# Where the edge columns of a transform are loaded and multiplied, in a kernel that overlaps an FFT mixer with an MLP

## The chip, the cores and the metric

The kernel runs on one core of one Trainium2 chip. The metric is the time of one execution in device microseconds (us). A core has five engines that run their own instruction streams: TensorE (PE) multiplies matrices, with its weight loads (PEld) beside it; VectorE (DVE), ScalarE (ACT) and GpSimd (POOL) do elementwise work and copies; SyncE (SP) issues transfers. ScalarE and GpSimd issue transfers too, and each issue takes its place in that engine's stream. Transfers between memory and the on-chip buffers are done by 16 DMA engines. Matmul results land in PSUM and are copied from there by ScalarE or VectorE.

## The reference

What is computed is a gated mix of two branches and the gradients of all its inputs but one. Cut to what matters:

```python
def _A_ref(x, w_r, w_i):                      # spectral branch
    X = rfft2(x.astype(float32)) * (w_r + 1j * w_i)
    return irfft2(X, s=(S, D)).astype(bfloat16)

def _B_ref(x, w1, b1, w2, b2):                # MLP branch
    h = relu(x @ w1 + b1)
    return (h * h) @ w2 + b2

g = sigmoid((x * gate_w).sum(-1, keepdims=True))
out = g * _A_ref(x, w_r, w_i) + (1 - g) * _B_ref(B_x, w1, b1, w2, b2)
# outputs: out, and the vjp with grad_out for A_x, A_w_r, A_w_i, B_w1, B_b1, B_w2, B_b2, gate_w
```

S = 2048 rows, D = 1024 columns, F = 3584 hidden units, bfloat16. The MLP branch is far the larger part; the spectral branch, forward and backward, is done in three stages of matmuls against constant matrices, and these are put in among the MLP's matmuls.

## The kernel before

Python generators write the program. `mlp_grads` writes the weight gradients: 7 groups of 512 hidden units for one weight, 7 for the other, each group 8 products of 16 matmuls (`pw`), one `yield` after each product. `fft_mid` (second stage of the transform: along the rows, the product with the spectral weights, and back) and `fft_out` (third stage) yield after each of their pieces, and `spread` puts these pieces between the products:

```python
def spread(main, side, per_main, start=0.0):
    due, done = start, 0
    for _ in main:
        due += per_main
        while done < due:
            next(side, None)
            done += 1
        yield

def spectra():
    yield from fft_mid()
    yield from fft_out()

spec, grads = spectra(), mlp_grads()
next(grads), next(grads)
todo = 9 + 6 * (R1 // 2) + 2 * NT
for _ in spread(grads, spec, todo / (2.0 * FG * FGC * NH - 2)):
    pass
```

A product of `mlp_grads` (line 816 of the kernel is the `mm`, line 820 the copy):

```python
pw = mps.tile([P, H], FP32, name="pw", tag="pw", bufs=2)
for t in range(NT):
    mm(pw[:], lhsT=cur[:, t, fb_ * P : (fb_ + 1) * P], rhs=dbn[:, t, hf * H : (hf + 1) * H],
       start=(t == 0), stop=(t == NT - 1))
last = nc.scalar.copy(out=wo[:, hf * H : (hf + 1) * H], in_=pw[:])
```

The second stage of the transform begins with the loads of its constants and of the first rows. `ld` issues on SyncE's queue, `st` on GpSimd's:

```python
ld, st = nc.sync.dma_start, nc.gpsimd.dma_start
...
am = fb.tile([P, NM, 2, P], FDT, name="am", tag="am")
ld(out=am[:], in_=cten["am"].ap())            # line 308, 1 MB
bm = fb.tile([P, NM, 2, P], FDT, name="bm", tag="bm")
ld(out=bm[:], in_=cten["bm"].ap())            # line 310, 1 MB

def inputs(m):                                # rows of the pair m, and their spectral weights
    z = fb.tile([P, 2, 2, H], FDT, name="z", tag="z", bufs=2)
    for n, c in enumerate((m, R1 // 2 + m)):
        for x in range(2):
            ld(out=z[lanes[x], n], in_=z_scr[:][c, :, x ^ n if m else x])     # line 316
    wn = ...                                  # four more ld, lines 320
    return z, wn
```

One column in 512 cannot be handled with its row pair and is treated by itself, for all 16 pairs at once: the edge columns. They are loaded element by element (16 pairs x 64 rows, one float16 each, per load), arranged, multiplied in 32 small matmuls with 4 columns, and put into place in `x` of each pair later:

```python
def edges():
    ed = ...; low = ...; mid = ...            # [P, NM, 2, 4], [P, NM, 4], [P, 4]
    col = z_scr[:].rearrange("c r x t l -> r c (x t) l")[:, :, :, 0]
    for e in range(4):
        nc.scalar.dma_start(out=ed[lanes[0], :, 0, e], in_=col[:, 0:NM, e])     # line 341
        nc.scalar.dma_start(out=low[lanes[1], :, e], in_=col[:, NM:, e])        # line 342
    nc.scalar.dma_start(out=mid[lanes[0]], in_=col[:, NM])                      # line 343
    nc.vector.tensor_copy(out=ed[lanes[0], :, 1, :], in_=ed[lanes[0], :, 0, :])
    nc.vector.tensor_copy(out=ed[lanes[0], 0, 1, :], in_=mid[lanes[0]])         # line 345
    ...                                       # four more small copies from low, lines 348, 349
    nc.vector.memset(ed[lanes[1], 0], 0.0)                                      # line 350
    sp = tps.tile([P, NM, 2, 4], FP32, name="sp", tag="tr", bufs=2)
    for m in range(NM):
        for n in range(2):
            mm(sp[:, m, n], lhsT=am[:, m, n, :], rhs=ed[:, m, n, :], ...)       # line 354
    ex = ...                                  # four copies out of sp, line 358
    return ex

def transform(m, n, pm, x):
    px = fps.tile([P, 2, H], FP32, name="px", tag="ps2", bufs=2)
    for T in range(2):
        mm(px[:, T, :], lhsT=am[:, m, n, :], rhs=pm[:, n, T, :], start=True, stop=True)  # line 375
    ...                                       # two copies out of px on ScalarE

nxt = inputs(0)
ex = edges()
pm, w = mirrored(0, nxt[0]), by_groups(nxt[1])
nxt = inputs(1)
held = gs = None
for _ in range(3):
    yield
for m in range(NM + 1):
    if m < NM:
        x = fb.tile([P, 2, 2, LW], FDT, name="x", tag="x", bufs=2)
        for n in range(2):
            transform(m, n, pm, x)
            yield
        nc.vector.tensor_copy(out=x[:, :, :, 0::H], in_=ex[:, m])               # line 473
    ...                                       # products with the weights, back transform (pv), outputs
```

The third stage, `fft_out`, works on tiles of 128 rows: load `r` (ScalarE's queue), `rf` on VectorE, matmuls `pki`, copy `rt`, matmuls `pui`, and elementwise work that ends in `ax_scr`. The `grp` tiles of the weight gradients are loaded with transposing transfers on SyncE's queue.

Of the kernel before, what the change touches and what calls it, by code (L numbers as in the profile page):

```python
# [135 lines left out]
def kernel(  # L136
# [22 lines left out]
    nc = tc.nc  # L159
# [8 lines left out]
    R1, R2 = g.R1, g.R2  # L168
    NT = S // P
# [8 lines left out]
    ld, st = nc.sync.dma_start, nc.gpsimd.dma_start  # L178
# [11 lines left out]
    def pool(name, side="left", space=SBUF, stack=None, bufs=1):  # L190
        stack = ExitStack() if stack is None else stack
        kw = {} if space == DRAM else dict(side=side, reuse_waits="tile")
        return stack.enter_context(tc.tile_pool(name=name, bufs=bufs, space=space, **kw)), stack

    pers, _ = pool("pers", stack=ctx)
    dram, _ = pool("dram", space=DRAM, stack=ctx)
# [105 lines left out]
    def fft_mid():  # L302
        fb, fbs = pool("f2", "right")
        NM, G = R1 // 2, nc.gpsimd
        lanes = [slice(R2 * n, R2 * (n + 1)) for n in range(2)]
# [6 lines left out]
        def inputs(m):  # L312
# [3 lines that stand above are left out]
                    ld(out=z[lanes[x], n], in_=z_scr[:][c, :, x ^ n if m else x])  # L316
            wn = fb.tile([P, 2, LW], BF16, name="wn", tag="wn", bufs=2)
            for c_, src_w in enumerate((A_w_r, A_w_i)):
                for n, k in enumerate(pair_of(m, R1)):
                    ld(out=wn[lanes[n], c_, 0:W1], in_=every(src_w, k))  # L320
            return z, wn

        def by_groups(wn):

            w = fb.tile([P, 3, LW], BF16, name="w", tag="w", bufs=2)
            G.tensor_copy(
                out=w[:, 0:2, 0:H].rearrange("p c (g i) -> p c g i", g=4),
                in_=wn[:, :, 0:H].rearrange("p c (i g) -> p c g i", g=4),
            )
            G.tensor_copy(out=w[:, 0:2, H], in_=wn[:, :, H])  # L330
            G.tensor_scalar(out=w[:, 2, 0:W1], in0=w[:, 1, 0:W1], scalar1=-1.0, scalar2=None, op0=ALU.mult)
            return w

        def edges():

            ed = fb.tile([P, NM, 2, 4], FDT, name="ed", tag="ed")
            low = fb.tile([P, NM, 4], FDT, name="low", tag="low")
            mid = fb.tile([P, 4], FDT, name="mid", tag="mid")
            col = z_scr[:].rearrange("c r x t l -> r c (x t) l")[:, :, :, 0]
            for e in range(4):  # L340
                nc.scalar.dma_start(out=ed[lanes[0], :, 0, e], in_=col[:, 0:NM, e])  # L341
                nc.scalar.dma_start(out=low[lanes[1], :, e], in_=col[:, NM:, e])
            nc.scalar.dma_start(out=mid[lanes[0]], in_=col[:, NM])
            nc.vector.tensor_copy(out=ed[lanes[0], :, 1, :], in_=ed[lanes[0], :, 0, :])
            nc.vector.tensor_copy(out=ed[lanes[0], 0, 1, :], in_=mid[lanes[0]])
            for n in range(2):
                a, b = slice(2 * n, 2 * n + 2), slice(2 - 2 * n, 4 - 2 * n)
                nc.vector.tensor_copy(out=ed[lanes[1], :, n, a], in_=low[lanes[1], :, a])
                nc.vector.tensor_scalar(out=ed[lanes[1], :, n, b], in0=low[lanes[1], :, b], scalar1=-1.0, scalar2=None, op0=ALU.mult)
            nc.vector.memset(ed[lanes[1], 0], 0.0)  # L350
# [3 lines that stand above are left out]
                    mm(sp[:, m, n], lhsT=am[:, m, n, :], rhs=ed[:, m, n, :], start=True, stop=True, skip_group_check=True)  # L354
            ex = fb.tile([P, NM, 2, 2, 2], FDT, name="ex", tag="ex")
            for n in range(2):
                for c in range(2):
                    nc.vector.tensor_copy(
                        out=ex[lanes[n], :, c], in_=sp[lanes[c], :, n, :].rearrange("p m (e t) -> p m t e", e=2)
                    )  # L360
            return ex

        def mirrored(m, z):

            if m == 0:
                return z
            pm = fb.tile([P, 2, 2, H], FDT, name="pm", tag="pm", bufs=2)
            V(out=pm[:, 0], in0=z[:, 0], in1=z[:, 1], op=ALU.add)
            V(out=pm[:, 1], in0=z[:, 0], in1=z[:, 1], op=ALU.subtract)
            return pm  # L370
# [4 lines that stand above are left out]
                mm(px[:, T, :], lhsT=am[:, m, n, :], rhs=pm[:, n, T, :], start=True, stop=True)  # L375
            for c in range(2):
                nc.scalar.copy(out=x[lanes[n], c, :, 0:H], in_=px[lanes[c]])  # L377
# [28 lines left out]
        def back(m, y, ye):  # L406
            pc = fb.tile([P, 2, 2, H], FDT, name="pc", tag="pc", bufs=2)
            for n in (1, 0):
                pv = fps.tile([P, 2, H], FP32, name="pv", tag="ps2", bufs=2)
                for T in range(2):  # L410
                    mm(pv[:, T, :], lhsT=bm[:, m, n, :], rhs=y[:, n, T, 0:H], start=True, stop=True)  # L411
                if m == 0:
                    nc.scalar.copy(out=pc[:, n], in_=pv[:])
                elif n == 1:
                    vc = fb.tile([P, 2, H], FP32, name="vc", tag="vc")
                    nc.scalar.copy(out=vc[:], in_=pv[:])
                else:
                    V(out=pc[:, 0], in0=pv[:], in1=vc[:], op=ALU.add)
                    V(out=pc[:, 1], in0=pv[:], in1=vc[:], op=ALU.subtract)
                yield  # L420

            sp = tps.tile([P, 2, 2], FP32, name="si", tag="tr", bufs=2)
            for n in range(2):
                mm(
                    sp[:].rearrange("p a t -> p (a t)"), lhsT=bm[:, m, n, :], rhs=ye[:, n].rearrange("p a t -> p (a t)"),
                    start=(n == 0), stop=(n == 1), skip_group_check=True,
                )
            nc.vector.tensor_copy(out=pc[lanes[1], 0, :, 0], in_=sp[lanes[0], 0, :])
            if m:
                nc.vector.tensor_copy(out=pc[lanes[0], 1, :, 0], in_=sp[lanes[1], 1, :])  # L430
            else:
                nc.vector.tensor_copy(out=pc[lanes[1], 1, :, 0], in_=sp[lanes[0], 1, :])
            for n, c in enumerate((m, R1 // 2 + m)):
                for h in range(2):
                    st(out=y_scr[:][c, :, h ^ n if m else h], in_=pc[lanes[h], n])
# [22 lines left out]
                    st(out=every(dst_w, k), in_=gw[lanes[n], c_, 0:W1])  # L458

        nxt = inputs(0)  # L460
        ex = edges()
        pm, w = mirrored(0, nxt[0]), by_groups(nxt[1])
        nxt = inputs(1)
        held = gs = None
# [2 lines left out]
        for m in range(NM + 1):  # L467
            if m < NM:
                x = fb.tile([P, 2, 2, LW], FDT, name="x", tag="x", bufs=2)
                for n in range(2):  # L470
                    transform(m, n, pm, x)
                    yield
                nc.vector.tensor_copy(out=x[:, :, :, 0::H], in_=ex[:, m])
            if held:
                backs = back(m - 1, *held)
                next(backs)
                yield
            if m < NM:
                ts = products(x, w)
            if held:  # L480
                next(backs)
                grads_out(m - 1, gs)
                yield
                for _ in backs:
                    pass
            if m < NM:
                held = joined(m, *ts)
                yield
                gs = grads_of_w(x)
                if m + 1 < NM:  # L490
                    pm, w = mirrored(m + 1, nxt[0]), by_groups(nxt[1])
                if m + 2 < NM:
                    nxt = inputs(m + 2)
                for _ in range(1 if m else 3):
                    yield
# [764 lines left out]
# [3 lines that stand above are left out]

    spec, grads = spectra(), mlp_grads()
    next(grads), next(grads)
    todo = 9 + 6 * (R1 // 2) + 2 * NT
    for _ in spread(grads, spec, todo / (2.0 * FG * FGC * NH - 2)):
        pass
    tps_s.close()
# [45 lines left out]
```

## Time and profile before

| | |
|---|---|
| time, median of three executions | 1284.11 us (1283.38 to 1285.54) |
| span of the profiled execution | 1283.1 us |
| ScalarE, busy | 503.4 us (39%) |
| VectorE, busy | 709.3 us (55%) |
| edge loads: number, to landing (`ed`, median) | 9, 3.8 us |
| edge matmuls: number, duration of one (median) | 32, 166 ns |
| first `pw` matmul of the weight gradients | 446.56 us |

The profile page gives each engine's busy time and a strip of 40 slices of the span, with one digit of busy tenths for each slice (9 is 90% or more) and one for the clock that TensorE was granted. The list of waits names, for each instruction that had its engine idle, what ended the idle time. The timeline lists instructions in order of start, neighbours of one kind merged. Matmuls of TensorE overlap, so a single one lasts 379 ns in the trace while the next begins about 216 ns after it.

### The profile page before, as it was taken

How to read it: one execution, taken by the hardware profiler on the slowest of the kernel's cores; microseconds unless marked ns; L12 is line 12 of the kernel's file. 1: busy time of each engine (PE TensorE's matmuls, PEld its weight loads, DVE VectorE, ACT ScalarE, POOL GpSimd, SP SyncE). 2: the span in 40 equal slices, each digit the busy share in tenths (PEclk: the TensorE clock that was granted, in tenths of full speed). 3: DMA queues.
4: the chain of work that ended last, by engine and by line, in shares of the span. 5: the costliest groups of instructions: out<-in, count | busy, mean ns of one | idle time of the engine just before them, and what ended most of it. 6: DMA issues, size and time to landing. Idle time of an engine off the chain costs nothing.

```text
span 1283.1 us, 18411 instructions
## 1 busy us (share of the span) xinstructions
PE 1257.8 (98%) x6884; PEld 610.0 (48%) x6884; DVE 709.3 (55%) x1602; ACT 503.4 (39%) x793; POOL 273.2 (21%) x424
## 2 busy tenths in 40 slices
PE   9999999999999979999999999999999999999997
PEld 5555544555544434444444444455445444444443
DVE  3554433544482206766765762343776776896573
ACT  4756654666633314554555552344111211011100
POOL 0111111111100115545545632122010010000000
PEclk9999999999999989999999999999999999999999
DMA  9566353546454679998778669995899877566540
GB/s 287 202 182 181 132 156 124 178 149 189 104 136 113 154 182 199 222 267 199 186 180 191 134 165 260 256 250 180 223 233 215 211 189 207 155 187 181 162 117 33
DMA packets 326260, 233.27 MB, mean 182 GB/s; under 512 B 195308, under 2 KB 279434, under 8 KB 325914
## 3 DMA queue, kind: packets, MB, share of 16 engines
q1 hardware_dynamic: 282528, 141.17, 47.0%
q0 software_dynamic: 26144, 82.47, 19.3%
q10 hardware_dynamic: 17498, 8.45, 2.7%
q8 instruction: 54, 0.88, 0.3%
q14 instruction: 36, 0.29, 0.1%
HBM read 106.19 MB, written 81.81 MB: 147 GB/s over the span
## 4 chain that ended last, share of the span: by engine, by line
PE 61%; DVE 4%; DMA 2%; issue 1%; ACT 1%; ACTq 1%; SPq 0%; DVEq 0%
PE pw L832 14%; PE acc L906 14%; PE pw L816 12%; PE xX L1015 7%; PE xV L1015 3%; PE pd L685 3%; PE ph L675 3%; PE xZ L1015 2%; DMA grp<-dhT_scr 1%; PE pui L294 1%; PE pki L529 1%; PE px L375 1%; PE pv L411 1%; ACTq L341 1%; ACT x L377 0%
## 5 line engine op out<-in xcount | busy, mean ns | idle before, releaser
L675 PE MATMUL ph<-xT,w1g 128*128 128x512 bf16 x896 | 221.1, 379 | 1.2 <-DMA w1g<-in_B_w_dram 1.2
L685 PE MATMUL pd<-dbT,w2T 128*128 128x512 bf16 x896 | 211.3, 379 | 0.4 <-DVE dhT L689 0.4
L816 PE MATMUL pw<-dbn,grp 128*128 128x512 bf16 x896 | 202.6, 382 | 0.9 <-ACT wo L820 0.4
L832 PE MATMUL pw<-grp,res 128*128 128x512 bf16 x896 | 200.9, 379 | 0.0
L906 PE MATMUL acc<-w,hblk 128*128 128x512 bf16 x896 | 198.7, 379 | 0.0
L689 DVE SCALAR_TENSOR_TENSOR dhT<-pd,rT 128x512 bf16<-128x512 f32 x112 | 77.4, 691 | 202.9 <-PE pd L685 162.9
L816 PEld LDWEIGHTS <-grp 128*128 128x128 bf16 x896 | 87.3, 98 | 108.1 <-issue 6.4
L685 PEld LDWEIGHTS <-w2T 128*128 128x128 bf16 x896 | 87.1, 98 | 103.4 <-issue 1.2
L906 PEld LDWEIGHTS <-hblk 128*128 128x128 bf16 x896 | 86.3, 98 | 98.0
L832 PEld LDWEIGHTS <-res 128*128 128x128 bf16 x896 | 86.0, 98 | 98.3
L675 PEld LDWEIGHTS <-w1g 128*128 128x128 bf16 x896 | 84.6, 98 | 90.4 <-DMA w1g<-in_B_w_dram 1.5
L677 ACT ACTIVATE rT<-ph,b1col 128x512 bf16<-128x512 f32 x112 | 77.0, 687 | 116.4 <-PE ph L675 116.4
L974 ACT ACTIVATE g<-gatew_bc,dsc 128x1024 f32<-128x1024 bf16 x16 | 18.3, 1148 | 147.3 <-DVE gxo L1024 120.6
L837 ACT CAST wo<-pw 128x512 bf16<-128x512 f32 x56 | 32.7, 585 | 102.3 <-PE pw L832 48.0
L678 ACT ACTIVATE h2T<-rT 128x512 bf16<-128x512 bf16 x112 | 70.6, 630 | 2.5
L1015 PEld LDWEIGHTS <-dS 128*128 128x128 f16 x448 | 43.8, 98 | 53.3 <-DVE dS L1003 0.5
L820 ACT CAST wo<-pw 128x512 bf16<-128x512 f32 x56 | 32.5, 583 | 91.9 <-PE pw L816 56.4
L531 ACT CAST rt<-pki 128x1024 f16<-128x1024 f32 x32 | 32.5, 1015 | 89.0 <-PE pki L529 80.9
L377 ACT CAST x<-px 64x1024 f16<-64x1024 f32 x64 | 64.4, 1006 | 0.7
L283 POOL DMA_DIRECT2D z_scr<-u x32 | 23.2, 726 | 171.2 <-ACT u L278 101.4
L730 POOL DMA_DIRECT2D h2T_scr<-h2T x28 | 20.3, 727 | 182.9 <-ACT h2T L678 167.3
L558 POOL DMA_DIRECT2D ax_scr<-yo x32 | 17.3, 540 | 170.8 <-DVE yo L557 156.1
(189 smaller groups left out, 1618.0 us busy)
## 6 DMA issues: line engine op xcount, KB each, us to landing
h2T_scr<-h2T POOLq DMA_DIRECT2D x28, 512.0 KB, 4.2
dhT_scr<-dhT POOLq DMA_DIRECT2D x28, 512.0 KB, 4.6
hblk<-h2T_scr SPq DMA_DIRECT2D x16, 896.0 KB, 6.3
hblk<-dhT_scr SPq DMA_DIRECT2D x16, 896.0 KB, 8.4
z_scr<-u POOLq DMA_DIRECT2D x32, 256.0 KB, 3.1
z<-z_scr SPq DMA_DIRECT2D x64, 128.0 KB, 3.3
y_scr<-pc POOLq DMA_DIRECT2D x64, 128.0 KB, 3.3
r<-y_scr ACTq DMA_DIRECT2D x32, 256.0 KB, 5.2
```

The source lines that it names most:

```text
L377: nc.scalar.copy(out=x[lanes[n], c, :, 0:H], in_=px[lanes[c]])
L531: nc.scalar.copy(out=rt[n][:], in_=pk[:])
L675: mm(ph[:], lhsT=w1g[:, dc, fc % 2 * P : (fc % 2 + 1) * P], rhs=xT[:, dc, ss], start=(dc == 0), stop=(dc == DC - 1))
L677: nc.scalar.activation(rT[:], ph[:], ACT.Relu, bias=b1col[:, fc : fc + 1])
L678: nc.scalar.activation(h2T, rT[:], ACT.Square)
L685: mm(pd[:], lhsT=w_[:, ec, fc % FGC * P : (fc % FGC + 1) * P], rhs=dbT[:, ec, ss], start=(ec == 0), stop=(ec == DC - 1),)
L689: return STT(out=dhT, in0=pd[:], scalar=2.0, in1=rT[:], op0=ALU.mult, op1=ALU.mult, accum_out=gb1part[:, fc, sb : sb + 1],)
L816: mm(pw[:], lhsT=cur[:, t, fb_ * P : (fb_ + 1) * P], rhs=dbn[:, t, hf * H : (hf + 1) * H], start=(t == 0), stop=(t == NT - 1),)
L832: mm(pw[:], lhsT=xr[t][:, d_ * P : (d_ + 1) * P], rhs=cur[:, t, :], start=(t == 0), stop=(t == NT - 1),)
L837: nc.scalar.copy(out=wo[:], in_=pw[:])
L906: turn["PE"] = mm(acc[:], lhsT=cur[:, fc, t2 * P : (t2 + 1) * P], rhs=w2[:, fc, cs], start=(fc == 0), stop=(fc == FC - 1))
L1015: mm(acc[:], lhsT=lhs[:, fc, :], rhs=rhs[:, fc, :], start=start and fc == 0, stop=fc == KH - 1, skip_group_check=True,)
```

## The change

The nine edge loads go from ScalarE's queue to SyncE's. The function is cut in two: `edges` only issues the loads, in the place where they were, after the loads of the first pair; `edges_through`, with the small copies, the 32 matmuls and the copies of their results, is called later, once the first pair's two forward transforms are written and three empty turns have gone by. `todo`, the number of turns that sets the rate of the interleaving, grows by the four turns that this adds. The purpose is that TensorE meets the edge matmuls when their inputs are there, and that ScalarE does not spend time on issuing the loads. No arithmetic changes.

```diff
@@ in edges
             for e in range(4):
-                nc.scalar.dma_start(out=ed[lanes[0], :, 0, e], in_=col[:, 0:NM, e])
-                nc.scalar.dma_start(out=low[lanes[1], :, e], in_=col[:, NM:, e])
-            nc.scalar.dma_start(out=mid[lanes[0]], in_=col[:, NM])
+                ld(out=ed[lanes[0], :, 0, e], in_=col[:, 0:NM, e])
+                ld(out=low[lanes[1], :, e], in_=col[:, NM:, e])
+            ld(out=mid[lanes[0]], in_=col[:, NM])
+            return ed, low, mid
+
+        def edges_through(ed, low, mid):
             nc.vector.tensor_copy(out=ed[lanes[0], :, 1, :], in_=ed[lanes[0], :, 0, :])
@@ in fft_mid
         nxt = inputs(0)
-        ex = edges()
+        edge = edges()
         pm, w = mirrored(0, nxt[0]), by_groups(nxt[1])
@@ in the loop over pairs
                 for n in range(2):
                     transform(m, n, pm, x)
+                    yield
+                if m == 0:
+                    for _ in range(3):
+                        yield
+                    ex = edges_through(*edge)
                     yield
                 nc.vector.tensor_copy(out=x[:, :, :, 0::H], in_=ex[:, m])
@@ at the interleaving
-    todo = 9 + 6 * (R1 // 2) + 2 * NT
+    todo = 13 + 6 * (R1 // 2) + 2 * NT
```

## The prediction

> **What bounds the kernel now.** I read the busy shares and the 40-slice strip first, then the list of TensorE's waits, then the timeline around the largest of them, then the waits of SyncE's queue and the DMA queues in that stretch.
>
> The page says that TensorE (PE) is the bound, and its clock strip says where it is disturbed:
>
> ```profile
> PE 1257.8 (98%) x6884; PEld 610.0 (48%) x6884; DVE 709.3 (55%) x1602; ACT 503.4 (39%) x793; POOL 273.2 (21%) x424
> ...
> PE   9999999999999979999999999999999999999997
> ...
> PEclk9999999999999989999999999999999999999999
> ```
>
> Only 25.3 of 1283.1 us are without a matmul. In the middle of the run one slice, the 15th (449 to 481 us), is low in both strips. The waits of TensorE, longest first, name the cause:
>
> ```profile
> PE sp L354 <- DVE ed L350: 8.2, 1, 8.2
> PE pki L529 <- ACT rt L531: 2.5, 1, 2.5
> PE ph L675 <- DMA w1g<-in_B_w_dram: 1.2, 1, 1.2
> ```
>
> `sp` is the target of the 32 edge matmuls. They make one wait of 8.2 us; everything else in the kernel is small beside it. The timeline of that stretch, cut (start, duration, engine, line, instruction, count, and in brackets the idle time before it and what ended it):
>
> ```profile
> 446.56 10.52 PE L816 MATMUL pw<-dbn,grp 128*128 128x512 bf16 x48
> ...
> 447.15 0.43 SPq L310 DMA_DIRECT2D bm<-c_bm  x1
> ...
> 452.06 4.97 ACTq L341 DMA_DIRECT2D ed<-z_scr  x1
> ...
> 459.92 3.35 SPq L316 DMA_DIRECT2D z<-z_scr  x4
> 459.99 0.58 ACT L820 CAST wo<-pw 128x512 bf16<-128x512 f32 x1 [9.18 <-DMA ed<-z_scr]
> ...
> 465.34 0.16 PE L354 MATMUL sp<-ed,am 128*128 128x4 f16 x1 [8.25 <-DVE ed L350]
> ...
> 466.57 0.97 PE L354 MATMUL sp<-ed,am 128*128 128x4 f16 x31 [0.62 <-DVE ed L345]
> ...
> 467.40 8.61 PE L816 MATMUL pw<-dbn,grp 128*128 128x512 bf16 x31
> ```
>
> Two things are to be seen. TensorE gets through 48 weight-gradient matmuls, meets the edge matmuls, and stops, because the nine loads of single columns are late. And ScalarE, which issues those loads, cannot copy a finished product out of PSUM for 9.18 us. The last line hides a third cost: 31 matmuls that take 6.7 us at the usual distance (see below) take 8.6.
>
> SyncE's queue is held up too. Its largest wait in the stretch 440 to 490 us after that for the first constant is
>
> ```profile
> SPq L316 <- DMA ed<-z_scr: 12.8, 2, 12.3
> ```
>
> so the first pair's `z` loads sit behind the edge loads: in the program's instruction lists every load waits for the load that held its completion semaphore before, eight of them go round over both queues, and here an edge load holds the one `z` wants.
>
> **What the Trainium skill says.** *TensorE: Matmul & The Clock Gate*, "Part 1: The HAM clock gate": after an idle window of about 3.4 us the array runs at half clock until it has been busy for about as long. The trace agrees: in the timeline of weight loads the first ones after the wait are 0.42 to 0.43 us apart (468.21, 468.63, 469.06, ...) up to about 471.1, against 10.52 us for 48 (and its drain), or 3.45 us for 16, i.e. 0.216, before it. *DMA: Bandwidth & Descriptors*, "Rules for kernel authors": a load whose last dimension is strided becomes one descriptor per element. The trace agrees: between 446 and 476 us ScalarE's queue moved 0.02 MB in
>
> ```profile
> q10 hardware_dynamic: 8592, 0.02, 16.3%
> ```
>
> 8592 packets; eight loads of 64 x 16 elements and one of 64 x 4 are 8448 elements. The same page, "Issuing engines are not separate DMA queues": loads from either queue end up on the same 16 engines, and only the issuing engine's time is saved. So I expect the move to SyncE's queue to free ScalarE and to change the order of the loads, not to make the element-wise loads cheaper; that the slowest `ed` load landed 8.1 us after its issue, beside `am` and `bm`, and the median one 3.8 us, fits.
>
> **The change, part by part.**
>
> 1. *What stands where on TensorE.* The two programs' instruction lists give, from the first `pw` on: before, 48 `pw`, 1 `sp`, 1 `pw`, 31 `sp`, 31 `pw`, 2 `px`, 16 `pw`, 2 `px`. After: 80 `pw`, 2 `px`, 16 `pw`, 2 `px`, 48 `pw`, 32 `sp`. The number of matmuls is the same. The edge matmuls move back by 48 + 48 = 96 `pw` and 4 `px`.
>
> 2. *What the stop costs.* Before, the last of 96 `pw`, 32 `sp` and 4 `px` ends its slot at 479.73 + 2 x 0.216 = 480.16 us, 33.6 us after 446.56. At the undisturbed pace these are 100 wide matmuls x 0.2157 = 21.6 us and 32 `sp` at 0.83 us (31 of them ran from 466.57 to 467.40), together 22.4. The difference, 11.2 us, is all that can be won here. By parts: 8.25 + 0.62 of waiting; 31 `pw` in 8.45 us (467.40 to 475.85, where the pair `px` starts) where 31 x 0.2157 = 6.7 would do, 1.8 us of low clock; the single `pw` between, 0.2; 0.3 of small gaps. Sum 11.2.
>
> 3. *Are the first forward transforms in time?* They move ahead: 446.56 + 80 x 0.2157 = 463.8 us (before 475.85). They need `am` and `z` of the first pair. In the changed list `z` follows `bm` on SyncE's queue and takes semaphores whose holders are long done, so it can be issued from 447.6 us and not from 459.92. Its 0.5 MB, and 0.26 MB of `wn`, line up behind `am` and `bm` (1 MB each) and the two stores of 0.5 MB that are still under way. The DMA strip shows 320 to 440 GB/s from 449 us on and the 3 MB gone by about 457; 0.5 MB more at 400 GB/s is 1.3 us, and some 2 us to be reported: about 460. Margin some 3 us. This is the tightest step.
>
> 4. *Are the edge loads in time?* They come after the eight loads of the first pair, each held until `z` or `wn` has landed on its semaphore, so from about 460 us. Nine issues of 0.7 us (the ScalarE issues were 0.66 to 0.81, but for one of 4.97) end at 466; the median landing of `low` is 4.6 us, which gives 470.5, and seven small VectorE operations of 0.06 to 0.18 us end at 472. The edge matmuls stand at 463.8 + 4 x 0.216 + 64 x 0.2157 = 478.5. Margin 6 us: the wait is gone.
>
> 5. *ScalarE* loses nine issues, 10.9 us from 450.45 to 461.4, and copies its products in time. ScalarE is 39% busy, so this alone moves nothing.
>
> 6. *What is added.* No instruction that works: four more resumptions of the side work in the interleaving, matched by 13 for 9 in `todo`. The side work advances 141/110 = 1.282 steps per group of 16 matmuls instead of 137/110 = 1.245, so it is 3% denser and its third stage starts at the same distance from the end. Between 475.85 and 758 us TensorE was busy 281.3 of 282.2 us, so there is room for a little delay at its inputs. I allow 0.7 us for new short waits.
>
> Sum: 1284.1 - 11.2 + 0.7 = 1273.6 us.
>
> **Rivals.** *(a) The wait moves.* If `z` lands late, TensorE stops at the first forward transform at 463.8 instead. For it: `am`, `bm` and two stores saturate the DMA engines just then, and one ScalarE issue hung for 4.97 us in the same jam; SyncE's could too. Against it: that hang ended at 457.07, with the jam. Waiting 2 to 5 us there gives 1276 to 1279, and only with a longer stop does the clock fall again. *(b) The edge loads hold up what follows on SyncE's queue.* The second pair's `z`, and the transposing loads of `grp`, now stand behind nine issues of 6.3 us. Against it: `z` of the second pair was issued at 466.86 before and would be at about 467 now, because the queue starts 12 us earlier; its transform stands some 14 us after the edge matmuls. Were it late, 1275 to 1280. *(c) The new rhythm meets a wait elsewhere.* The 2.5 us wait of `pki` on `rt` comes from `r` loads caught between transposing loads; the shifted order can remove it or lengthen it: plus or minus 2 to 3 us. *(d) The gain is not passed on,* because DMA sets the later pace: then 1280 or more. Against it: TensorE has no DMA wait over 1.2 us in the list.
>
> **Range and chances.** The centre is the sum, 1273.6. Downward only the `pki` wait and small gaps remain, 3 us: low 1270. Upward (a), (b) or (c) adds up to 5 us: high 1278.5. A gain over 2% is 25.7 us, which is all of TensorE's idle time and out of reach: 0.01. A loss over 2% needs a new stop three times the old one: 0.01. Within 2%: 0.98.
>
> **What would show it right or wrong.** Right: the waits of TensorE no longer name `sp`; the strip of the clock has no low slice in the middle; `px` starts near 463.8 and the 32 `sp` run together near 478.5; TensorE's busy time falls by about 2 us (low clock counts as busy) and its idle time by about 9. Wrong: a wait of `px` on a `z` load near 464 us (step 3), of `sp` on `ed` near 478 (step 4), or a longer wait of `pm`, `grp` or `pki` later (step 6).

## The result, and the profile after

The changed kernel takes 1274.46 us (median, 1274.18 to 1276.15); the kernel before took 1284.0 us beside it. The ratio is 0.9924 [0.9905, 0.9943]: a gain of 0.76%, which lies within the 2% that counts as the same. The profiled executions, on which all that follows rests, have spans of 1283.1 and 1272.8 us, 10.3 us apart.

The page of the changed kernel, TensorE's busy time and the clock strip:

```profile
PE 1249.1 (98%) x6753; PEld 609.6 (48%) x6884; DVE 706.4 (56%) x1602; ACT 503.7 (40%) x793; POOL 270.9 (21%) x424
...
PEclk9999999999999999999999999999999999999999
```

The low slice is gone from the clock strip. The busy time must be read with care: this trace has 6753 matmul records where the weight loads number 6884, so 131 records are missing and the printed 1249.1 us is too small. The clock strip and the waits can be used; busy and idle time of TensorE cannot.

The top of TensorE's list of waits (instruction waiting, what it waited for, us in total, times, longest):

```profile
PE ph L683 <- DMA w1g<-in_B_w_dram: 1.2, 1, 1.2
PE pz L1182 <- DVE zeros L1175: 1.2, 1, 1.2
PE pw L840 <- ACT wo L845: 1.1, 2, 0.6
```

`sp` and the 2.5 us of `pki` on `rt` have left the top; nothing over 1.2 us remains. The timeline of the stretch, cut (start, duration, engine, line, instruction, count):

```profile
446.63 17.43 PE L824 MATMUL pw<-dbn,grp 128*128 128x512 bf16 x79
...
452.33 4.60 SPq L320 DMA_DIRECT2D wn<-in_A_w_i_dram  x2
...
457.57 0.63 SPq L341 DMA_DIRECT2D ed<-z_scr  x1
...
463.90 0.59 PE L378 MATMUL px<-z,am 128*128 128x512 f16 x2
...
478.58 0.95 PE L357 MATMUL sp<-ed,am 128*128 128x4 f16 x32
...
479.39 13.97 PE L824 MATMUL pw<-dbn,grp 128*128 128x512 bf16 x62
```

The line of `wn` is two issues of 0.47 us; the 3.7 us between them are a wait of SyncE for the load of `bm`. TensorE goes through its 80 weight-gradient matmuls (one record is missing) into the first pair's transforms without a bracket of idle time, and the 32 edge matmuls run as one group. At 479.39 us, where the next `pw` starts, TensorE has done the same matmuls that it had done at 490.5 us in the kernel before: there the second pair of `px` was followed at 480.17 us by

```profile
480.17 6.21 PE L816 MATMUL pw<-dbn,grp 128*128 128x512 bf16 x28
```

and 48 `pw` at 0.2157 us end at 490.52. Counted from the first `pw`, that is 32.8 us where it was 44.0: the stretch gave 11.2 us. The first matmul into `acc`, a later stage, came at 894.2 us and comes at 883.4, 10.8 us earlier; the end comes 10.3 us earlier. So the gain is made in one place, and 0.9 us of it is lost on the rest of the way.

### The profile page after: what moved, and what is told of

Read it like the earlier page. It is cut to its first block, busy times and chain, and to the rows that moved or that the text cites. A ratio compares the mean times of both kernels' runs of the same rounds, so it can differ in the third digit from the quotient of the medians.

```text
span 1272.8 us, 18282 instructions
## 1 busy us (share of the span) xinstructions
PE 1249.1 (98%) x6753; PEld 609.6 (48%) x6884; DVE 706.4 (56%) x1602; ACT 503.7 (40%) x793; POOL 270.9 (21%) x424
## 4 chain that ended last, share of the span: by engine, by line
PE 61%; DVE 4%; DMA 2%; issue 2%; ACT 1%; POOL 0%; SPq 0%; ACTq 0%; DVEq 0%; POOLq 0%
PE acc L914 14%; PE pw L824 13%; PE pw L840 12%; PE xX L1023 7%; PE xV L1023 3%; PE pd L693 3%; PE ph L683 3%; PE xZ L1023 2%; PE pui L294 1%; PE pki L537 1%; PE px L378 1%; PE pv L414 1%; DMA r<-y_scr 1%; DMA out_dram<-wo 1%; ACT x L380 1%
## 5 line engine op out<-in xcount | busy, mean ns | idle before, releaser
L683 PE MATMUL ph<-xT,w1g 128*128 128x512 bf16 x864 | 216.9, 379 | 2.7 <-DMA w1g<-in_B_w_dram 1.2
L824 PE MATMUL pw<-dbn,grp 128*128 128x512 bf16 x876 | 198.9, 379 | 1.9 <-ACT wo L828 0.7
```

Of the source, the lines that this page charges most:

```text
L683: mm(ph[:], lhsT=w1g[:, dc, fc % 2 * P : (fc % 2 + 1) * P], rhs=xT[:, dc, ss], start=(dc == 0), stop=(dc == DC - 1))
```

## The experiments

The theory: the change removes one stop of TensorE, with the low clock that follows it, and both halves of the change are needed: the queue so that ScalarE is free, the deferral so that the loads have time. One rival: the new rhythm of the side work (`todo` and the empty turns) is what helps. Another: moving the loads to SyncE alone would do. A third: the loads have a cost of their own, which the change only hides in part. Each time is a median with the ratio to the kernel before, run beside it on the same chip. A trace shows one execution; for three of the kernels below (the queue alone, the deferral alone, the queue with `pm` reordered) it is one that took 2.3 to 3.2 us longer than the kernel's median, so a single wait in it need not be in every execution (those of the queue alone go from 1276.07 to 1283.5 us).

### The queue alone

```diff
-                nc.scalar.dma_start(out=ed[lanes[0], :, 0, e], in_=col[:, 0:NM, e])
+                ld(out=ed[lanes[0], :, 0, e], in_=col[:, 0:NM, e])
  (and the same for low and mid; nothing else)
```

> Only the nine edge loads move to SyncE's queue; the edge function stays whole and is called where it was, todo stays 9. In the instruction lists this alone already moves the edge matmuls: 80 pw, 2 px, 13 pw, 1 sp, 2 pw, 31 sp. Theory (the gain is the edge matmuls standing late enough for their loads): they stand at 446.6 + 80 x 0.2157 + 0.43 + 13 x 0.2157 = 467.1 us, and their inputs are ready at about 470.1 as in the changed kernel, so TensorE waits some 3 us for sp, too short for the low clock: 1284.0 - 11.2 + 3.0 = 1276 us, with no px wait. Rival (the queue is what brings the gain, by freeing ScalarE and letting z go first; the later place adds nothing): 1274 us, no wait of sp over 0.5 us. Second rival (the later place is everything and the queue nothing): 1284 us.

Measured: 1280.36 us, 0.9961 [0.9945, 0.9977]. The edge matmuls wait 2.1 us, near the 3 expected. Two things were not. The clock falls although the wait is so short. The trace in stretches (columns: stretch; its length; busy time and count of PE, PEld, DVE, ACT and POOL; granted clock; DMA share; GB/s):

```profile
467.00:469.00 2.00, 0.11 (x1) 0.10 (x1) 0.36 (x3) 0.00 (x0) 0.00 (x0) 1.00 0.64 108
469.00:470.00 1.00, 0.75 (x3) 0.27 (x3) 0.30 (x3) 0.00 (x0) 0.00 (x0) 0.66 0.65 195
470.00:472.00 2.00, 2.00 (x35) 1.28 (x34) 0.84 (x4) 0.43 (x1) 0.00 (x0) 0.50 0.62 133
```

TensorE is idle from 467.1 to 469.25 and works at half clock from then until about 472.6. And a new wait has come 40 us later, for ScalarE's copy `wo`:

```profile
511.11 6.57 PE L816 MATMUL pw<-dbn,grp 128*128 128x512 bf16 x16 [3.50 <-ACT wo L820]
```

From the first of these 16 matmuls to the next instruction, `pv` at 517.51 us, 6.40 us pass, where 3.45 would do (16 x 0.2157). The kernels without empty turns, below, ask where this wait comes from. The queue alone gives 0.4%, about half of the gain.

### The deferral alone

```diff
@@ the changed kernel, with the loads put back
-                ld(out=ed[lanes[0], :, 0, e], in_=col[:, 0:NM, e])
+                nc.scalar.dma_start(out=ed[lanes[0], :, 0, e], in_=col[:, 0:NM, e])
  (and the same for low and mid)
```

> As the changed kernel, but the nine edge loads stay on ScalarE's queue. The TensorE list is that of the changed kernel. Theory: the inputs of sp are there at 466.6 as before and sp stands at 478.5, so no wait of sp; but z of the first pair again follows the edge loads on their shared semaphores, is issued at about 459.9 and lands at about 464, where px stands at 463.8: a px wait of 0 to 2 us, and ScalarE's copy of a product again held some 9 us; two PSUM buffers of pw then make TensorE wait for that copy, because the matmuls no longer stop: 48 pw are three products and the held copy is the second, so the fourth product waits for it from 457 to about 460.6, some 3.5 us. Sum 1284.0 - 11.2 + 4 to 5.5 = 1277 to 1278 us. Rival (deferral is everything): 1274 us, as the changed kernel.

Measured: 1279.49 us, 0.9958 [0.9941, 0.9975]. The transforms are in time, and so are the edge matmuls. Another matmul stops, the fourth product as expected, and this timeline of ScalarE and TensorE says why:

```profile
462.19 0.59 ACT L828 CAST wo<-pw 128x512 bf16<-128x512 f32 x1 [9.73 <-DMA ed<-z_scr]
...
462.83 7.46 PE L824 MATMUL pw<-dbn,grp 128*128 128x512 bf16 x26 [4.08 <-ACT wo L828]
```

ScalarE issues the nine loads and is held 9.73 us; its copy of a product out of PSUM comes late, and TensorE has no buffer to go on with. In the kernel before the same hold of ScalarE (9.18 us) cost nothing, because TensorE was standing anyway. This is what the move of the queue is for. The 1.5 to 2.5 us by which the expectation was too low is mostly the low clock after the wait, which it had not counted: from 464 to 467 us the clock is 0.50 and the matmuls start 0.43 us apart. The 32 `pw` from 462.83 us to `px` at 471.42 take 8.59 us, where 6.90 would do, so some 1.7 us are lost.

### The gap filled with useless matmuls

If TensorE is kept busy while it waits for the edge loads, the wait stays and only the low clock is taken away. Two kernels do this with matmuls whose result nobody reads; they do more work than the kernel before.

```diff
@@ the kernel before, ahead of the edge matmuls
+            fill = fps.tile([P, 2, H], FP32, name="fill", tag="ps2", bufs=2)
+            for _ in range(40):                     # 50 in the second
+                mm(fill[:, 0, :], lhsT=dbn[:, 0, 0:P], rhs=dbn[:, 1, 0:H], start=True, stop=True)
```

> The kernel before, with 40 matmuls of no use written ahead of the edge matmuls (operands from the gradient tile, result never read); 36 to 40 of them stand in the gap, 8 us at 0.216. Nothing is loaded earlier. Theory: the wait costs twice, by itself and by the half clock after it; with the gap filled the clock does not fall, so the 31 pw after sp take 6.7 us instead of 8.5 and the kernel becomes about 2 us faster although it does more work: 1282 us, no low slice in the clock strip. Rival (the slow matmuls after the stop have another cause, such as transfers): 1284 us or above, and the matmuls after sp still 0.427 us apart.

Measured with 40: 1282.42 us, 0.998 [0.9969, 0.9992]. The time is as expected and the reason is not. The filler ran out too early: `sp` still waited 0.56 and 0.89 us. The clock fell all the same. The same columns as above, of this kernel:

```profile
465.70:468.10 2.40, 0.95 (x33) 0.88 (x33) 0.48 (x4) 0.00 (x0) 0.00 (x0) 1.00 0.76 148
468.10:470.00 1.90, 1.90 (x12) 0.68 (x9) 0.89 (x4) 0.00 (x0) 0.56 (x1) 0.55 0.54 152
```

In 2.40 us TensorE was busy for 0.95, with matmuls of four columns, and the clock was then halved. The second `px` came at 480.56 us (before: 479.73), so nothing was won here; in the profiled execution the gain came later, most of it because the `pki` wait of 2.5 us happened not to occur. So I filled more.

> As e3 with 50 useless matmuls for 40, 46 of them in the gap, so that they end at about 467.7 us, after the inputs of sp are there (467.3). In e3 TensorE still waited 0.6 and 0.9 us and the clock still fell, for 9 matmuls after sp. Theory: low use of the array in the 2.4 us of small matmuls and short waits is what lowers the clock; without the waits it stays high, the 32 pw after sp take 6.9 us and not 8.6, and the time is 1.3 us below e3: 1281.1 us although ten matmuls are added. Rival (the small sp matmuls alone lower the clock, or the slow matmuls have another cause): 0.427 us between matmuls after sp again, 1283 to 1284 us.

Measured with 50: 1280.94 us, 0.9967 [0.9954, 0.9979]. Now the edge matmuls do not wait, and the next `pw` run at full clock. The two kernels, with 40 and with 50 (one record is missing in the first):

```profile
468.09 8.75 PE L819 MATMUL pw<-dbn,grp 128*128 128x512 bf16 x31
476.68 0.59 PE L378 MATMUL px<-z,am 128*128 128x512 f16 x2
```

```profile
468.08 7.07 PE L819 MATMUL pw<-dbn,grp 128*128 128x512 bf16 x32
474.98 0.59 PE L378 MATMUL px<-z,am 128*128 128x512 f16 x2
```

From the first filler to the first `px` takes 28.86 us, where the kernel with 40 took 30.14: ten matmuls more (2.2 us of work) in 1.28 us less. Of these 3.4 us, 1.45 are the two waits; of the other 2.0, the low clock is 1.7 (8.59 against 6.90 us for the 32 `pw`), near the 1.8 of the prediction. The filled gap is still a lost one.

### Without the empty turns

```diff
                 if m == 0:
-                    for _ in range(3):
-                        yield
                     ex = edges_through(*edge)
                     yield
@@
-    todo = 13 + 6 * (R1 // 2) + 2 * NT
+    todo = 10 + 6 * (R1 // 2) + 2 * NT
```

> The changed kernel without the three empty turns (todo 10 for 13): sp stands right behind the second px, at about 468.2 us, its inputs are ready at about 470.1. Theory: TensorE waits some 1.9 us for sp, no low clock: 1274.5 + 1.9 = 1276.4 us. Rival (the empty turns are not needed, or only change the rhythm): 1274.5 us, no wait of sp over 0.5 us.

Measured: 1281.8 us, 0.9973 [0.9961, 0.9985], 5.4 us more than expected. At the edge matmuls it went as the theory says: they wait 1.4 us, and the clock stays at 1.00 after it. The rest is one wait, 37 us later, and the timeline lets it be followed back through four engines:

```profile
490.44 3.13 SPq L316 DMA_DIRECT2D z<-z_scr  x4
...
496.65 0.69 DVE L371 TENSOR_TENSOR pm<-z 128x1024 f16<-128x1024 f16 x1 [11.94 <-DMA z<-z_scr]
...
503.89 1.96 ACT L455 ACTIVATE gw<-gs 128x1024 bf16<-128x1024 f16 x1 [8.79 <-DVE gs L454]
...
506.37 5.33 PE L822 MATMUL pw<-dbn,grp 128*128 128x512 bf16 x15 [5.01 <-ACT wo L826]
```

SyncE issues the `z` loads of pair 3 only at 490.44, because its queue has been issuing four transposing loads of `grp` from 477.84 on, 12.5 us. VectorE reaches `pm` of pair 3 (the sums and differences of its rows), which needs that `z`, and stands there for 11.94 us. Behind it, in VectorE's order, are the pieces of pair 1 that are ready: the copy into `x`, and after more steps `gs` (for the gradient of the spectral weights). ScalarE waits for `gs` and has the copy `wo` behind it. TensorE waits for that copy, 5.01 us, and from there to the next `px` at 511.75 us its 16 matmuls (one record is missing) take 5.38 us where 3.45 would do. In the changed kernel the same `pm` waits too, but pair 1 is later there: its `x` is ready only at 498.03, so nothing on VectorE is held up.

```profile
496.18 0.69 DVE L371 TENSOR_TENSOR pm<-z 128x1024 f16<-128x1024 f16 x1 [6.53 <-DMA z<-z_scr]
...
498.03 0.18 DVE L481 COPY x<-ex 128x8 f16<-128x8 f16 x1 [0.55 <-ACT x L380]
```

On this reading the empty turns do a second job that nothing in the diff tells of: they keep pair 1 behind a load that is late anyway. To test this chain, I kept the empty turns out and had `pm` written behind `gs` on VectorE.

```diff
@@ in mirrored, and the same for pm[:, 1]
-            V(out=pm[:, 0], in0=z[:, 0], in1=z[:, 1], op=ALU.add)
+            after(V(out=pm[:, 0], in0=z[:, 0], in1=z[:, 1], op=ALU.add), done.get(m - 2), NoSync)
@@ in grads_of_w, where gs of a pair is made
-            V(out=gs[:, 1, 0:W1], ...)
+            done[len(done)] = V(out=gs[:, 1, 0:W1], ...)
```

> As e4 (no empty turns), and on VectorE the sums pm of pair m are kept behind the gradient difference gs of pair m-2, an order alone. TensorE's list is that of e4. In e4 TensorE waited 5.0 us near 506 us for ScalarE's copy of a product, with half clock after it; I trace that to pm of pair 3, which stands ahead of pair 1's work on VectorE and waits until 496.6 us for a z load that stands behind the transposing grp loads on SyncE's queue. Theory: with pm out of the way the 5.0 us wait and the low clock after it (2 us) vanish, and what is left above the changed kernel is the 1.4 us wait of sp: 1281.8 - 7 = 1275 us. Rival (the copy is late for another reason, such as ScalarE's own load or the DMA engines under the transposes): the wait near 506 us stays, 1281 to 1282 us.

Measured: 1280.9 us, 0.9977 [0.9964, 0.999]. The wait near 506 us is gone, as the chain demands, and the time is still 6 us above the expectation. `pw` now waits twice for longer, with smaller waits between:

```profile
596.82 3.61 PE L824 MATMUL pw<-dbn,grp 128*128 128x512 bf16 x16 [2.29 <-ACT wo L828]
...
691.84 5.30 PE L840 MATMUL pw<-grp,res 128*128 128x512 bf16 x16 [2.28 <-ACT wo L845]
```

The 16 matmuls after the second wait run in part at the low clock, those after the first do not. The edge matmuls wait 1.42 us, and here the low clock does follow: the 64 `pw` after them take 15.42 us to the next `px`, in the kernel without that order 13.81. The same order put into the kernel with the queue alone:

> As e1 (loads on SyncE's queue, nothing deferred), with the same order of pm on VectorE as in e5. TensorE's list is that of e1. e1 waited 3.5 us near 511 us for ScalarE's copy and ran 15 matmuls at half clock after it (3.2 us). Theory: both vanish, the 2.1 us wait of sp stays: 1280.4 - 6.7 = 1273.7, so 1273 to 1276 us; the queue move with an undisturbed VectorE is then worth as much as the whole change. Rival (the deferral itself is needed): 1278 us or more.

Measured: 1281.65 us, 0.9976 [0.9965, 0.9988], against 1273 to 1276 expected. The wait at 511 us is gone here too, but six on `wo` (5.5 us together) and one of 3.7 us of `pki` on `rt` stand in the list. And in the changed kernel, where no wait was there to be removed:

> The changed kernel with the same order of pm on VectorE. There pm of pair 3 also waits 6.5 us for its load, but x of pair 1 is ready only 1.4 us after it goes on, so it costs nothing. Theory: no difference, 1274.5 us within 0.7. Rival (some of the short waits of pv and pw that the changed kernel has at 480 to 760 us, 1.6 us in all, come from pm too): 1273 us or below, and then this is the best version.

Measured: 1280.02 us, 0.9958 [0.9942, 0.9975], so the order costs some 5 us by itself: the fastest execution, 1278.44 us, lies above the slowest of the changed kernel, 1276.15. Its list of VectorE's waits, and then that of the changed kernel, show what it does:

```profile
DVE x L483 <- ACT x L382: 93.0, 15, 7.8
```

```profile
DVE pm L371 <- PE px L378: 44.8, 11, 5.8
DVE x L481 <- ACT x L380: 31.3, 15, 7.5
```

In the changed kernel VectorE waited 31.3 us for `x` and 44.8 us for the transforms ahead of `pm`: it made `pm` in the gaps. Held back for every pair, `pm` can no longer be made in these gaps, its first half comes to stand between `gs` and the small scaling of `gs` that ScalarE waits for, and TensorE waits for `wo` five times, 5.1 us. So the order costs time by itself when it holds for every pair, and these three runs leave open what the chain costs. The reordering should concern only the pair whose `z` is late.

```diff
@@ the kernel without empty turns and with the order, and the same for pm[:, 1]
-            after(V(out=pm[:, 0], ...), done.get(m - 2), NoSync)
+            after(V(out=pm[:, 0], ...), (done.get(1) if m == 3 else None), NoSync)
```

> As e5, but only pm of pair 3 is kept behind pair 1's gs on VectorE; the other pairs are as in e4. In e5 the wait near 506 us was gone, but keeping every pair back gave new waits for the copy of a product (2.3 us near 597 and 692, with low clock after the second), because pm of the later pairs came late. Theory: without those the kernel comes to e4 less the 5.0 us wait and 2 us of low clock, 1281.8 - 7 = 1275 us (1274.5 to 1277). Rival (any shift of the order costs some 5 us of waits somewhere): 1279 us or more.

Measured: 1273.7 us, 0.9901 [0.987, 0.9932], a little below the expected range and 8 us below the kernel without empty turns. Pair 3 alone was the trouble there:

```profile
468.77 1.11 PE L357 MATMUL sp<-ed,am 128*128 128x4 f16 x32 [0.61 <-DVE ed L353]
```

The edge matmuls wait 0.61 us, with no low clock after it, and `pw` waits 1.2 us in all in place of 6.2. The empty turns can be left out once the order is right. It is not shown to be faster than the change: the two intervals overlap.

### The rhythm alone

```diff
@@ the kernel before
-        for _ in range(3):
+        for _ in range(7):
             yield
@@
-    todo = 9 + 6 * (R1 // 2) + 2 * NT
+    todo = 13 + 6 * (R1 // 2) + 2 * NT
```

> The kernel before with the four more turns (put into the empty turns ahead of the first pair) and todo 13, edge loads and edge matmuls as before. Theory (the gain comes from the edge wait alone): the stop of 8 us with the low clock after it stays where it was; the 2.5 us wait of pki may go and some 3 us of short waits may come, as in the changed kernel: 1284 us within 1.5. Rival (the denser rhythm brings part of the gain): 1281 us or less.

Measured: 1285.34 us, 1.0003 [0.9986, 1.0021]. The stop stays, and with it the low slice of the clock strip:

```profile
PE sp L354 <- DVE ed L350: 7.2, 1, 7.2
```

The `pki` wait on `rt` has gone, to no gain. The denser rhythm gives nothing by itself; the first rival falls.

### No edge loads at all

This kernel leaves the nine loads out and clears their tiles instead, so the edge columns of the transforms are missing from its output.

```diff
@@ the changed kernel
-            for e in range(4): ... ld(...)          # the nine loads
+            for t_ in (ed, low, mid):
+                nc.vector.memset(t_[:], 0.0)
```

> The changed kernel with the nine edge loads left out and their tiles cleared instead, so that the edge columns of the result are missing. Theory (the edge loads are hidden altogether): no gain over the changed kernel, 1274.5 us within 1; z of the second pair is issued 9 us earlier, to no use. Rival (the loads still cost time, by holding SyncE's queue or the DMA engines): 1272 us or less.

Measured: 1273.98 us, 0.9904 [0.9873, 0.9935], against 1274.46 for the changed kernel; the two intervals overlap, and 1272 or less was expected had the loads kept a cost. So no cost that is left of them can be measured; the third rival falls.

### A slower rhythm

```diff
-    todo = 13 + 6 * (R1 // 2) + 2 * NT
+    todo = 11 + 6 * (R1 // 2) + 2 * NT
```

> The changed kernel with todo 11 for 13, so the side work advances 1.264 steps per product instead of 1.282. The edge matmuls stand where they stand in the changed kernel. Theory: the edge gain of 11.2 us is kept; what differs is which copies and loads meet TensorE later, 3.4 us of waits between 480 and 880 us in the changed kernel: 1272 to 1278 us. If it is below 1274 it is the better version. Rival (the rhythm after the edges does not matter): 1274.5 us within 0.5.

Measured: 1275.7 us, 0.9918 [0.9886, 0.995]. The edge matmuls stay in time (478.44 us, no wait). `pki` waits 2.7 us for `r` and 0.9 for `rt`. The median lies 1.2 us above that of the changed kernel and the intervals overlap, so the time alone does not show that the rhythm matters. The waits show that a small shift moves single ones by as much as the two or three microseconds of the prediction's rival (c).

## Why the prediction was right

Predicted were 1273.6 us; 1274.46 was measured, and the mechanism is the one predicted.

- **Step 1, the order,** is what the trace shows: 80 `pw`, then `px`, and the 32 `sp` together.
- **Step 2, what the stop costs,** was the number that carried the prediction. The stretch gave 11.2 us of 11.2, and all waits and the low clock in it are gone. Of its parts, the low clock was confirmed by the two filled kernels. The two kernels that do one half each show that neither half removes the stop alone: one leaves a shorter wait for `ed`, the other a wait for ScalarE.
- **Step 3, the first transforms:** predicted 463.8 us, seen 463.90, no wait. The first piece of `z`, issued at 447.69 us, took 9.9 us to land, and the last, issued at 450.1, landed 9.4 us later, at 459.5. That is near the 460 of the prediction, so the margin was 4.4 us. The sum there had 2 us for the report of a landing, which no run here shows by itself.
- **Step 4, the edge loads,** came out right with errors that offset each other, which is in part luck. They were issued from 457.57 us, not 460, when the first piece of `z` had landed and not the last. But nine issues took 9.8 us, not 6.3: I had reckoned 0.7 us apiece from ScalarE's issues, and two of SyncE's took 2.75 and 1.55 us, with a few tenths between some. The last load then landed 3.1 us after its issue, not 4.6. Inputs were ready at 470.2 us against 472; `sp` ran at 478.58 against 478.5. With the queue moved and the order kept, the same loads were still 2.1 us late; with both they have 8 us to spare.
- **Step 5, ScalarE:** its copies `wo` come at 450.29, 453.74, 457.19 and 460.65 us, one for each 16 matmuls. "This alone moves nothing" fits the kernel before, where TensorE was standing anyway, and is too short as a statement on the change. With the deferral and without the move, ScalarE's hold costs 4.08 us of waiting and the low clock.
- **Step 6, the allowance:** 0.7 us for new short waits; 0.9 was lost after the stretch. The `pki` wait of 2.5 us (and short ones of 0.7) went, and 3.4 us of short waits came (`pw` 1.1 and 0.7, `pv` 0.9, `pki` 0.7), with some 0.5 us more after `acc`. That these nearly offset each other was not foreseen one by one and is luck; it lay inside the range.
- **The rivals.** (a) did not happen. SyncE's queue did stand in the jam, 3.7 us between two `wn` issues, but for another reason than the one feared: it waited for `bm`, which landed 9.2 us after its issue at 447.22, and the second `wn` was issued at 456.47. (b) did not cost time in the changed kernel, but the chain behind it is real: pair 3's `z` stands behind transposing loads on SyncE, and without the empty turns it costs 5 us of waiting and the low clock. I had looked at pair 2. (c) is there and small. (d) is excluded by the end, which moved by 10.3 us.
- **The marker "TensorE's busy time falls by about 2 us and idle time by about 9"** cannot be read off, because records are missing.

What was too simple is my reading of the clock. *TensorE: Matmul & The Clock Gate*, "Part 1: The HAM clock gate" in the Trainium skill, speaks of an idle window of about 3.4 us, and I took the low clock to follow long stops only. Here it fell after waits of 2.1 us (the queue alone) and 1.42 us (no empty turns, `pm` behind `gs` for every pair), and after 2.4 us in which TensorE was busy for 0.95 (the filled gap). It did not fall after edge waits of 1.4 us (no empty turns), 1.9 us (the queue with the order of `pm`) or 0.6 us, and of the two waits of 2.29 and 2.28 us shown above it followed only the second. So the length of a wait alone does not decide, and no shortest harmful wait can be read off. The page also says that the window runs free, so where a stop falls in it may decide; these runs fit that and do not prove it. The wait of 2.1 us cost about 1.2 us more: from 469.28 to 472.61 us TensorE ran six wide matmuls and 31 `sp` in 3.33 us, where 2.1 would do.

Left open is whether the move of the queue, with only pair 3 reordered, would come to the same 1274 us. It was not run.

## What to carry to other kernels

When late inputs stop the bounding engine, count the stop with what it drags behind it (here 8.9 us of waiting and 2.3 us of low clock and gaps), and ask of each half of a remedy what it leaves: one half left the matmuls waiting for the loads, the other for ScalarE's copies, and each gave 0.4 of the 0.76%. Queues that run in order pass a late load on to engines that never use it: follow a new wait back through all of them, and reorder only the instruction that waits, for reordering every one took away VectorE's useful gaps and cost 5 us. An empty turn in an interleaving may hold more than what it was put there for, so take it out alone and look 40 us further on.

## What the runs showed of the hardware

The issue of a load can itself take long while the DMA engines are full. In the kernel before, an `ed` issue of ScalarE took 4.97 us, in a stretch (452 to 457 us) in which the trace gives the DMA engines a busy share of 0.99 to 1.01; in the changed kernel one of SyncE's took 2.75. Others of the same load took 0.63 to 0.73 us. ScalarE ran no copy for 9.18 us, from 450.80 to 459.99, while it issued seven of its loads. Each of the four transposing loads of `grp` took 2.4 to 4.5 us to issue in the kernel without empty turns, and this is what delayed the `z` behind them. A merged line of the timeline can hide a wait, though: the 4.60 us of the two `wn` issues above are 2 x 0.47 us of issue and 3.7 us of waiting.

A low clock need not follow the wait at once: in the kernel with the deferral alone TensorE restarted at 462.83 us and was halved about 1.1 us later.
